# A two-pass third product for the half block of a Winograd matmul, with the operand sums moved to later steps

## The chip, the cores and the metric

The kernel runs on one core of a Trainium2 chip. A core has a matrix engine (TensorE, PE in the profile; its weight loads are PEld), a vector engine (VectorE, DVE), a scalar engine (ScalarE, ACT), GpSimd (POOL) and a sync engine (SP) that mostly issues DMAs. Each engine runs its own instructions in the order in which they are issued, and engines wait for each other through semaphores. The metric is the device time of one execution in microseconds (us), lower is better. The time before is the median of 3 runs.

## The reference, cut to what matters

```
xn = layernorm(x)                                     # x: (2048, 640)
A  = Cr @ (xn @ Dr.T) - Ci @ (xn @ Di.T)              # DFT over both axes, real part
h  = layernorm(xn)
u  = gelu(h.T @ w1 + b1)                              # (640, 1728)
y  = (u @ w2 + b2).T                                  # (2048, 640)
out = x + A + y
```

All inputs are fp32. The change lies in the last product, y = w2.T @ u.T: 2048 rows of output, 640 columns, and a contraction over 1728 = 13 blocks of 128 rows and half a block of 64.

## The kernel before, in words

**Three passes.** A fp32 operand a is split into a high part a_h (ScalarE, `high`, L138, rounding to the type that TensorE multiplies in one pass) and a low part a_l = a - a_h (VectorE, `low`, L141). A product is then three matmuls into the same PSUM bank (`three`, L149, L150, L152): w_h by m_h, w_h by m_l, w_l by m_h. If the low part of the weights is given as `None`, the third is left out.

**Winograd form.** Each large product is done as a 2 x 2 block product with seven multiplications instead of eight. In `row_steps` (L767) the weights A11, A12, A21, A22 come from HBM by DMAs on the SP queue, and the moving operands (combinations of the blocks B) lie ready in SBUF. VectorE forms four sums of the weights: S1 = A21 + A22, S2 = S1 - A11, S3 = A11 - A21, S4 = A12 - S2. The products, in the order of their steps: P1 (weights A11), P5 (S1), P6 (S2), P2 (A12), P7 (S3), P3 (S4), P4 (A22). One pass over these seven makes two row blocks of the result and is called a row step here. P1, P6, P7 and P4 add into one PSUM bank, P5 and P3 into a second, and P2 has a third; after each product the state of its bank is read out ("P1 out" is the reading after P1; L854 on ScalarE where it is copied, L841 on VectorE where it is added to what was read before). So P6 may begin only once P1 is out, P7 once P6 is out, P4 once P7 is out, P3 once P5 is out.

**The last product in two halves.** The contraction blocks 0 to 13 are paired as (f, f + 7). The first half (`down0`, 8 row steps) takes pairs 0 to 3, the second (`down1`, 8 row steps) pairs 4 to 6; its moving operand is called `sdown` in both, and its three pairs make 9 matmuls per product, 128x128 weights by 128x320. Block 13 has only 64 valid rows. The host gives its weights twice, in rows 0 to 63 and again in rows 64 to 127. For P2 and P4, whose second operand is zero in the missing rows, this is used ("stacked"): the weights' upper 64 rows hold the low part of the lower 64, the high part of the moving operand is repeated there and its low part is zero there, so that two passes do the work of three (8 matmuls instead of 9). `cut_piece` (L170) then makes two low operations, one of 64x128 that writes into the high tile and one of 128x256. `tail_rows` (L724) prepares the moving side once, as jobs in the first half. In S1 the upper rows of the last block need a copy of A21's (L789), since A22's are the repeated ones.

**Order.** Everything is issued in an order written out by hand, in turns (`turn_of`): turn i issues in this order the loads, the readings of product i - 1, the sums, the high part for product i + 2, extras, jobs, the low part for product i + 2, what is in `behind_lo`, and the matmuls of product i. `s0` is the turn of P1. Before, S1 and S3 are issued at turn s0 - 2 ahead of P1's low part, S2 at s0 - 1, S4 at s0 + 2. S1 has a slot of its own ("s"); S2 replaces A11, S3 replaces A21, S4 replaces A12. The first row step of the DFT product over the hidden axis (`s_hid`) already uses another order, the one of the `if s0 == s_hid` branch: S1 behind P1's low part at s0 - 2, S2 in the place of S1 at s0, S3 at s0 + 1, S4 at s0 + 2.

**The last row step** does not add to the output by DMA; it has the output rows loaded and adds them while reading out, so P1, P5 and P6 are read by VectorE (L850) instead of ScalarE, and P4 in two halves (L846).

Of the kernel before, what the change touches and what calls it, by code (L numbers as in the profile page):

```python
# [8 lines left out]
F32 = mybir.dt.float32  # L9
R32 = mybir.dt.float32r  # L10
BF16 = mybir.dt.bfloat16
AF = mybir.ActivationFunctionType
ALU = mybir.AluOpType

P = 128
# [6 lines left out]
TAIL = F - NF * P  # L22
# [47 lines left out]
def fnet_plus_mixer(  # L70
# [30 lines left out]
    nc = tc.nc  # L101
# [35 lines left out]
    def high(hi, src):  # L137
        nc.scalar.activation(hi, src, AF.Copy)  # L138
# [4 lines left out]
    def sub(to, a, b):  # L143
        nc.vector.tensor_sub(to, a, b)  # L144
# [20 lines left out]
    loads, sums, reads, extras, timed, behind_lo = (defaultdict(list) for _ in range(6))  # L165
# [558 lines left out]
    def tail_rows():  # L724


        v = []

        def get():
            v.append(place["x2"]()[P - TAIL :])  # L730
            nc.sync.dma_start(v[0], part_up[NF2 - 1][:TAIL])

        def piece(row, n):
            return v[0][:, row, n * H2 : (n + 1) * H2]

        def second(which, i):
            return moving["down1", 2][P - TAIL :, which, i, :]

        def job1():
            high(second(0, 1), piece(1, 0))  # L740
            sub(piece(0, 1), piece(0, 1), piece(0, 0))

        def job2():
            sub(piece(1, 1), piece(1, 1), piece(0, 1))
            sub(piece(1, 0), piece(1, 0), piece(1, 1))

        def job3():
            high(second(0, 5), piece(1, 0))
            nc.gpsimd.memset(second(1, 5).bitcast(F32), 0.0)

        return get, [(job1,), (job2,), job3]

# [14 lines left out]
    def row_steps(stage, nq, load_piece, at, end, bias=(None, None), base=None, earliest=0, each=None, aside={}, tail=False, stacked=()):  # L767
# [6 lines left out]
        s0, n = len(steps), nq * P  # L774
        raw, banks, held = {}, {}, {}

        def load(*names):
            for name in names:
                raw[name] = raw_slot(n)
                load_piece(raw[name], int(name[1]) - 1, int(name[2]) - 1)  # L780
# [47 lines left out]
        def read(i):  # L828
# [34 lines left out]
                    end(held["c"])  # L863
            return run

        for e, names in loads_of.items():
            loads[max(s0 + e, earliest)].append(lambda names=names: load(*names))
        if s0 == s_hid:


            operand[6] = "s"
            behind_lo[s0 - 2].append(first_sum)
            sums_of = {
                0: (lambda: sub(raw["s"], raw["s"], raw["A11"]),),
                1: (lambda: sub(raw["A21"], raw["A11"], raw["A21"]),),
                2: (lambda: sub(raw["A12"], raw["A12"], raw["s"]),),
            }
# [7 lines left out]
    def collect(c, ts):  # L885
        for i in range(2):
            nc.gpsimd.dma_start(out_rows[ts[i]], c[:, i, :], accum_op=ALU.add)

    def hidden(n, t, earliest):
        ts = (t, t + 4)  # L890

        def load_piece(to, i, j):
            c, b = divmod(ts[i], CH // P)
            nc.sync.dma_start(to.rearrange("p (j t) -> p j t", j=ND), y_part[j][c][:, :, b * P : (b + 1) * P])

        return row_steps("hid", ND, load_piece, ("ca", "cb")[n % 2], lambda c: collect(c, ts), earliest=earliest)

    def up(stage, r, at):
# [54 lines left out]
        if tail:  # L953
            aside += (7, 4)
        s0 = row_steps(
            f"up{stage}", 4, load_piece, at, end, earliest=s_up - 4, aside={i: by_dram(i) for i in aside}, tail=tail,
        )
        return s0

    def down(stage, t, at):  # L960
        f0, nq = (0, 4) if stage == 0 else (4, 3)
        ts = (t, t + NS // 2)
        last = stage == 1 and t == NS // 2 - 1

        def load_piece(to, i, j):
            f = f0 + NF2 * j
            nc.sync.dma_start(to, w2[ts[i], :, f * P : (f + nq) * P])

        def each(c, row, half, whole, at=slice(0, H2), queue=nc.sync):
            if whole:  # L970
                queue.dma_start(out_rows[ts[row]][:, half * H2 : (half + 1) * H2][:, at], c[:, at])

        held = []

        def before():

            held.append(place["v"]())
            for i in range(2):
                nc.sync.dma_start(held[0][:, i, :], out_rows[ts[i]])

        if last:
            loads[len(steps) - LOADS].append(before)
        bias = [b2_sb[:, i : i + 1] if stage == 0 else None for i in ts]
        return row_steps(
            f"down{stage}", nq, load_piece, at, lambda c: collect(c, ts), bias, (lambda: held[0]) if last else None,
            each=each if last else None, stacked=(2, 4) if stage else (),
        )


# [14 lines left out]
    s_hid = len(steps)  # L1004
# [29 lines left out]
    for t in range(NS // 2):  # L1034
        down(0, t, ("cb", "x1")[t % 2])
# [7 lines left out]
    for t in range(NS // 2):  # L1043
        down(1, t, ("ca", "cb")[t % 2])
# [88 lines left out]
```

## Time and profile before

| | |
|---|---|
| median of 3 runs | 875.51 us (875.5 to 876.32) |
| profiled execution, its own time | 875.92 us |
| its span | 874.2 us |
| TensorE busy | 869.0 us, 99%, 4924 matmuls |
| VectorE busy | 711.7 us, 81% |
| ScalarE busy | 530.2 us, 61% |
| GpSimd busy | 126.2 us, 14% |
| granted TensorE clock | 0.999 |

The page lists the busy time of each engine, the chain of work that ended last, and groups of instructions by line, operation and tile, with the mean of one and the idle time before them. A matmul's listed duration runs from its start to the end of its pipeline, so matmuls overlap in the list and their spacing is shorter than their duration. In a timeline each row has a start and a duration in us, the engine, the line, the operation, what it writes and reads, and in brackets how long its engine was idle before it and what ended that.

### The profile page before, as it was taken

What the parts mean: (1) busy time and instruction counts of PE and PEld (TensorE: products, weight loads), DVE (VectorE), ACT (ScalarE), POOL (GpSimd) and SP (SyncE); (2) the same over time, 40 slices, a digit from 0 to 9 for tenths busy, and PEclk for the clock granted to TensorE, in tenths of its full rate; (3) what the DMA queues carried; (4) which work ended last, traced back from release to release, by engine and by line L of the source; (5) the groups of instructions that cost most, each with busy time, mean ns of one, the idle gap of its engine ahead of it and who ended that gap; (6) DMA issues with size and microseconds to landing.
All of it is one profiled execution on the core that took longest, in us unless ns stands there. A gap on an engine that the chain in (4) does not pass through costs nothing.

```text
span 874.2 us, 13999 instructions
## 1 busy us (share of the span) xinstructions
PE 869.0 (99%) x4924; PEld 793.1 (91%) x4924; DVE 711.7 (81%) x1217; ACT 530.2 (61%) x960; POOL 126.2 (14%) x170
## 2 busy tenths in 40 slices
PE   9999999999999999999999999999999999999998
PEld 6888888888888888889999999999999999999998
DVE  7878878795887978788887787998678978897887
ACT  5746576764556566557565556675577766555553
POOL 0110100101121111222010101000212221111211
PEclk9999999999999999999999999999999999999999
DMA  7771554619385556869666756454678797766786
GB/s 270 231 266 76 194 203 132 242 59 357 54 219 92 163 119 133 208 92 195 168 127 166 156 139 196 162 177 138 142 170 181 169 244 193 190 136 133 151 173 139
DMA packets 86087, 147.64 MB, mean 169 GB/s; under 512 B 8512, under 2 KB 35904, under 8 KB 85760
## 3 DMA queue, kind: packets, MB, share of 16 engines
q1 hardware_dynamic: 64928, 95.80, 34.0%
q0 software_dynamic: 20800, 50.70, 30.6%
q8 instruction: 38, 0.62, 0.3%
q14 instruction: 33, 0.27, 0.1%
q10 hardware_dynamic: 288, 0.25, 0.1%
HBM read 99.96 MB, written 52.00 MB: 174 GB/s over the span
## 4 chain that ended last, share of the span: by engine, by line
PE 94%; DVE 3%; ACT 1%; DMA 1%; issue 1%; DVEq 0%; ACTq 0%
PE psum L149 30%; PE psum L150 30%; PE psum L152 29%; PE psum L477 5%; DVE piece L141 1%; DMA pieces<-y 1%; DVE pieces L144 0%; DMA x<-in_x 0%; ACT piece L138 0%; ACT n L259 0%; ACT x L259 0%; DVE pair L144 0%; DVE st L210 0%; DVE pieces L785 0%; DVE shid L141 0%
## 5 line engine op out<-in xcount | busy, mean ns | idle before, releaser
L141 DVE TENSOR_TENSOR piece<-pieces,piece 128x512 fp32r<-128x512 f32 (+2 forms) x524 | 350.1, 671 | 125.8 <-ACT piece L138 119.1
L138 ACT ACTIVATE piece<-pieces 128x512 fp32r<-128x512 f32 (+3 forms) x508 | 318.1, 627 | 212.0 <-PE psum L152 143.5
L150 PE MATMUL psum<-piece,n 128*128 128x512 f32 x504 | 196.4, 390 | 0.0
L149 PE MATMUL psum<-piece,n 128*128 128x512 f32 x504 | 196.2, 389 | 0.0
L152 PE MATMUL psum<-piece,n 128*128 128x512 f32 x504 | 196.1, 389 | 0.0
L149 PE MATMUL psum<-sup,piece 128*128 128x320 f32 x392 | 121.2, 310 | 0.0
L149 PE MATMUL psum<-sdown,piece 128*128 128x320 f32 x392 | 121.0, 309 | 0.0
L150 PE MATMUL psum<-sup,piece 128*128 128x320 f32 x392 | 120.9, 309 | 0.0
L150 PE MATMUL psum<-sdown,piece 128*128 128x320 f32 x392 | 120.9, 309 | 0.0
L152 PE MATMUL psum<-sup,piece 128*128 128x320 f32 x376 | 116.6, 310 | 0.0
L152 PE MATMUL psum<-sdown,piece 128*128 128x320 f32 x376 | 116.2, 309 | 0.0
L144 DVE TENSOR_TENSOR pieces<-pieces 128x512 f32<-128x512 f32 (+3 forms) x142 | 112.7, 794 | 2.6
L150 PEld LDWEIGHTS psum<-piece,n 128*128 128x128 f32 x504 | 94.6, 188 | 21.0 <-DVE piece L141 1.5
L149 PEld LDWEIGHTS psum<-piece,n 128*128 128x128 f32 x504 | 94.6, 188 | 19.9
L152 PEld LDWEIGHTS psum<-piece,n 128*128 128x128 f32 x504 | 94.6, 188 | 19.3
L152 PE MATMUL psum<-shid,piece 128*128 128x320 f32 x280 | 86.6, 309 | 0.1
L150 PE MATMUL psum<-shid,piece 128*128 128x320 f32 x280 | 86.5, 309 | 0.0
L149 PE MATMUL psum<-shid,piece 128*128 128x320 f32 x280 | 86.5, 309 | 0.0
L854 ACT ACTIVATE pair<-psum 128x320 f32<-128x320 f32 x102 | 44.5, 436 | 54.6 <-PE psum L152 49.8
L149 PEld LDWEIGHTS psum<-sup,piece 128*128 128x128 f32 x392 | 73.6, 188 | 0.6 <-ACT pairs L854 0.3
L149 PEld LDWEIGHTS psum<-sdown,piece 128*128 128x128 f32 x392 | 73.6, 188 | 0.2 <-ACT pair L852 0.2
L150 PEld LDWEIGHTS psum<-sup,piece 128*128 128x128 f32 x392 | 73.6, 188 | 0.0
(106 smaller groups left out, 1115.8 us busy)
## 6 DMA issues: line engine op xcount, KB each, us to landing
pieces<-in_dft_seq SPq DMA_DIRECT2D x128, 256.0 KB, 5.4
pieces<-in_w SPq DMA_DIRECT2D x88, 256.0 KB, 3.7
y<-c POOLq DMA_DIRECT2D x84, 256.0 KB, 6.1
out<-pair POOLq DMA_DIRECT2D x38, 320.0 KB, 5.3
pieces<-y SPq DMA_DIRECT2D x32, 320.0 KB, 3.9
pieces<-in_w SPq DMA_DIRECT2D x32, 192.0 KB, 3.1
out<-in_x SPq DMA_DIRECT2D x16, 320.0 KB, 7.1
up<-pair POOLq DMA_DIRECT2D x8, 640.0 KB, 3.2
```

What stands on the lines that cost most here:

```text
L138: nc.scalar.activation(hi, src, AF.Copy)
L141: nc.vector.tensor_sub(lo, src, hi.bitcast(F32))
L144: nc.vector.tensor_sub(to, a, b)
L149: nc.tensor.matmul(psum, wh, mh, start=first, stop=False, skip_group_check=True)
L150: nc.tensor.matmul(psum, wh, ml, start=False, stop=last and wl is None, skip_group_check=True)
L152: nc.tensor.matmul(psum, wl, mh, start=False, stop=last, skip_group_check=True)
L477: nc.tensor.matmul(banks[m, j], channels(k, j)[rows], w[cols], start=n == 0 and k == begin, stop=n == 2 and k == end, skip_group_check=True,)
L854: nc.scalar.activation(c, b, AF.Copy)
```

## The change

In `down1`, P3 becomes stacked too, beside P2 and P4. Three things go with it. On the moving side, `tail_rows` repeats the high part of P3's operand in the upper rows and clears its low part there. On the weight side, S4's upper rows in the last block must repeat its lower rows; A12's already do, so the upper rows of S2 in the last block are overwritten with its lower ones on ScalarE (`second_time`, 64x128, turn s0 + 1), after P6's parts have been cut from S2 and before S4 is formed. And the sums of `down1` take the order of the `s_hid` branch: S1 behind P1's low part, S2 in the place of S1 at turn s0 instead of in the place of A11 at s0 - 1, S3 at s0 + 1 instead of s0 - 2, S4 from the slot "s". The line numbers of the changed kernel are up to 8 higher.

```diff
         def job1():
             high(second(0, 1), piece(1, 0))
+            high(second(0, 2), piece(1, 1))
             sub(piece(0, 1), piece(0, 1), piece(0, 0))
...
         def job3():
             high(second(0, 5), piece(1, 0))
-            nc.gpsimd.memset(second(1, 5).bitcast(F32), 0.0)
+            for i in (2, 5):
+                nc.gpsimd.memset(second(1, i).bitcast(F32), 0.0)
...
+        if stacked:
+
+            def second_time():
+                last = raw["s"][:, n - P :]
+                nc.scalar.activation(last[TAIL:], last[:TAIL], AF.Copy)
+
+            extras[s0 + 1].append(second_time)
         for e, names in loads_of.items():
             loads[max(s0 + e, earliest)].append(lambda names=names: load(*names))
-        if s0 == s_hid:
-
+        if s0 == s_hid or stacked:
 
             operand[6] = "s"
             behind_lo[s0 - 2].append(first_sum)
             sums_of = {
                 0: (lambda: sub(raw["s"], raw["s"], raw["A11"]),),
                 1: (lambda: sub(raw["A21"], raw["A11"], raw["A21"]),),
                 2: (lambda: sub(raw["A12"], raw["A12"], raw["s"]),),
             }
...
-            each=each if last else None, stacked=(2, 4) if stage else (),
+            each=each if last else None, stacked=(2, 3, 4) if stage else (),
```

## The prediction

> **What bounds the kernel now.** First the page: the span, the busy times, the chain that ended last, and one costly group of the stage that is changed.
>
> ```profile
> span 874.2 us, 13999 instructions
> PE 869.0 (99%) x4924; PEld 793.1 (91%) x4924; DVE 711.7 (81%) x1217; ACT 530.2 (61%) x960; POOL 126.2 (14%) x170
> ...
> PE 94%; DVE 3%; ACT 1%; DMA 1%; issue 1%; DVEq 0%; ACTq 0%
> ...
> L152 PE MATMUL psum<-sdown,piece 128*128 128x320 f32 x376 | 116.2, 309 | 0.0
> ```
>
> TensorE carries the chain. The 309 ns of a matmul is not what removing one saves, since matmuls overlap. Second, then, the busy time in a stretch of the changed stage (columns: stretch, sum, then PE, PEld, DVE, ACT, POOL, clock, DMA):
>
> ```profile
> 810.00:820.00 10.00, 10.00 (x70) 10.00 (x69) 8.39 (x20) 5.67 (x14) 1.87 (x3) 1.00 0.81 159
> ```
>
> PE has no gap at the full clock, and VectorE is 84% busy: little room if its work comes in a chain. Third, the timeline of one row step, VectorE and then ScalarE (start, duration):
>
> ```profile
> 805.44 0.49 DVE L841 TENSOR_TENSOR pair<-psum,pair 128x320 f32<-128x320 f32 x1
> 805.84 0.55 DVE L785 TENSOR_TENSOR pieces<-pieces 128x384 f32<-128x384 f32 x1
> 806.42 0.22 DVE L789 COPY pieces<-pieces 64x128 f32<-64x128 f32 x1
> 806.68 0.56 DVE L144 TENSOR_TENSOR pieces<-pieces 128x384 f32<-128x384 f32 x1
> 807.16 0.55 DVE L141 TENSOR_TENSOR piece<-pieces,piece 128x384 fp32r<-128x384 f32 x1
> 807.63 0.48 DVE L841 TENSOR_TENSOR pair<-psum,pair 128x320 f32<-128x320 f32 x1
> 808.03 0.55 DVE L144 TENSOR_TENSOR pieces<-pieces 128x384 f32<-128x384 f32 x1
> 808.49 0.55 DVE L141 TENSOR_TENSOR piece<-pieces,piece 128x384 fp32r<-128x384 f32 x1
> 809.23 0.56 DVE L141 TENSOR_TENSOR piece<-pieces,piece 128x384 fp32r<-128x384 f32 x1 [0.18 <-ACT piece L138]
> 810.13 0.73 DVE L141 TENSOR_TENSOR piece<-pieces,piece 64x128 fp32r<-64x128 f32 x2 [0.34 <-ACT piece L138]
> 810.89 0.56 DVE L144 TENSOR_TENSOR pieces<-pieces 128x384 f32<-128x384 f32 x1
> ...
> 813.24 0.48 DVE L841 TENSOR_TENSOR pair<-psum,pair 128x320 f32<-128x320 f32 x1
> 813.74 0.73 DVE L141 TENSOR_TENSOR piece<-pieces,piece 64x128 fp32r<-64x128 f32 x2
> 814.38 0.49 DVE L841 TENSOR_TENSOR pair<-psum,pair 128x320 f32<-128x320 f32 x1
> ```
> ```profile
> 805.43 0.53 ACT L138 ACTIVATE piece<-pieces 128x384 fp32r<-128x384 f32 x1 [0.74 <-PE psum L152]
> ...
> 808.67 0.53 ACT L138 ACTIVATE piece<-pieces 128x384 fp32r<-128x384 f32 x1 [0.31 <-DVE pieces L144]
> 809.25 0.44 ACT L854 ACTIVATE pair<-psum 128x320 f32<-128x320 f32 x1
> ```
> ```profile
> 807.73 0.31 PE L149 MATMUL psum<-sdown,piece 128*128 128x320 f32 x1
> ```
>
> 805.44 and 814.38 are P7 out in two successive row steps: 8.94 us for 61 matmuls, 0.1466 us each. In order VectorE shows: P7 out, S1, its copy, S3, P1's low part, P3 out, S2, low parts of P5, P6, P2 (a pair), S4 and, further on, P2 out, P4's low pair, P7 out. ScalarE shows P1's high part, P6's high part, P1 out. 807.73 is P1's first matmul. So today S1, S3 and S2 are all made before P6's high part is asked for.
>
> **The change, part by part.**
>
> *Matmuls.* One third pass fewer in each of 8 row steps, with its weight load: 8 x 0.1466 = -1.17 us. A row step becomes 60 x 0.1466 = 8.80 us of PE. The Trainium skill, TensorE: Matmul & The Clock Gate, section Back-to-back issue gap, gives N/2.4 + 2.5 ns, which for 320 columns is 136 ns; by it the saving would be 1.09 us, and the measured spacing decides.
>
> *Setup.* One more high part (64x320) and one more fill, once, before the stage.
>
> ```profile
> L749 POOL MEMSET sdown<- x1: 687/687/687, 788.0 to 788.0; 64x320 f32 x1
> ```
> ```profile
> 798.44 0.86 POOL L887 DMA_DIRECT2D out<-pairs  x1 [9.73 <-DVE pairs L841]
> ```
> ```profile
> L138 ACT ACTIVATE sdown<-pairs x14: 461/727/733, 644.9 to 791.3; 128x640 fp32r<-128x640 f32 x9, 128x320 fp32r<-128x320 f32 x3, 64x320 fp32r<-64x320 f32 x2
> ```
>
> POOL's second 0.69 us comes ahead of output DMAs for which POOL idles 9.73 us anyway. ScalarE's extra 0.46 us falls before 791.3; it is 61% busy over the span, and the stage that first needs the result begins at about 799 (eight row steps of 8.94 before the last matmul at about 870.4). Both cost 0; without that cover, 1.15 us together. No DMA is added. The SP queue is passed by nothing: A12's next load overwrites A11, whose last reader comes a turn sooner.
>
> *ScalarE's new copy (64x128, 8 times).* Not in this trace. Above it lies 128x256; below it, what 128 columns add from one width to the next.
>
> ```profile
> L138 ACT ACTIVATE piece<-pieces 128x384 fp32r<-128x384 f32 x56 | 29.2, 522 | 20.6 <-PE psum L152 13.8 <-DVE pieces L144 3.4 <-ACT piece L138 2.6
> L138 ACT ACTIVATE piece<-pieces 128x256 fp32r<-128x256 f32 x4 | 1.6, 411 | 0.0
> ```
>
> 128 columns add 0.11, so 0.41 - 0.11 = 0.30 us; bounds 0.11 and 0.41. I take 0.30, the straight line through both rows. It waits for P6's low part, and queued behind it on ScalarE are P5 out, P7's high part, P6 out, P3's high part. S4, which needs the copy, starts 1.24 us after that low part ends (0.47 + 0.57 + 0.76 - 0.56, steps below), so at either bound the copy is hidden. Above 1.2 us it would hold S4.
>
> *The later sums.* This is what costs. S2 now overwrites S1's slot, so it can start only after P5's low part has read it, and P6's parts only after S2. A row step of the first product already has this order:
>
> ```profile
> 406.06 0.82 DVE L141 TENSOR_TENSOR piece<-pieces,piece 128x640 fp32r<-128x640 f32 x1 [0.15 <-ACT piece L138]
> 406.92 0.82 DVE L144 TENSOR_TENSOR pieces<-pieces 128x640 f32<-128x640 f32 x1
> 408.61 0.83 DVE L141 TENSOR_TENSOR piece<-pieces,piece 128x640 fp32r<-128x640 f32 x1 [0.86 <-ACT piece L138]
> ```
> ```profile
> 407.84 0.74 ACT L138 ACTIVATE piece<-pieces 128x640 fp32r<-128x640 f32 x1 [0.83 <-DVE pieces L144]
> 408.48 0.42 ACT L854 ACTIVATE pair<-psum 128x320 f32<-128x320 f32 x1
> ```
>
> S2 starts 0.03 after the low part's end, ScalarE 0.09 after S2, the low part 0.03 after ScalarE, and P1 out stands behind that high part. With 384 columns the steps form a closed loop over a row step, start to start: P1 low to S1 0.47 (the spacing of two unhindered operations, 807.16 to 807.63); S1 to copy 0.58; copy to P5's high part 0.22 + 0.09 = 0.31; to P5's low part 0.53 + 0.03 = 0.56; to S2 0.55 + 0.03 = 0.58; to P6's high part 0.55 + 0.09 = 0.64; to its low part 0.56; to S3 0.47; to P2's low pair 0.57 (behind 813.24 the pair waits for the whole operation); to S4 0.76; to P3's high part 0.56 + 0.09 = 0.65; to P3's low pair 0.55; to P2 out 0.64 (as 813.74 to 814.38; splitting P3's low part adds 0.17); to P4's pair 0.50; to P7 out 0.64; to the next P1 low 0.40. Sum 8.88 us against PE's 8.80.
>
> So the loop, not PE, sets the steady row step. P6 adds into P1's bank, so its first matmul waits for P1 out, and P1 out now stands behind P6's high part. Counted from P3's first matmul (17 before 807.73, so 805.24): P1's high part 0.19, its low part 0.56 later, P6's high part 3.14 later (the six steps above), P1 out 0.43 after that (408.48 - 407.84, less the 0.21 by which the high part is shorter), done 0.44 later: 4.76. P6 is due 34 matmuls on, at 4.98, its second matmul at 5.13. In the case at 863.86 below, the second matmul follows such an end by 0.38, which allows 5.14 here: just in time when the loop starts on time. The first row step has longer turns before it and loses nothing; the second uses up what slack there is; five to six later ones lose 0.08 each: **+0.4 us**.
>
> *The last row step.* Here P1, P5 and P6 are read out by VectorE (L850), in the same queue as the loop.
>
> ```profile
> 862.91 0.56 DVE L141 TENSOR_TENSOR piece<-pieces,piece 128x384 fp32r<-128x384 f32 x1 [0.19 <-ACT piece L138]
> 863.38 0.48 DVE L850 TENSOR_TENSOR pair<-psum,pair 128x320 f32<-128x320 f32 x1
> ...
> 865.88 0.49 DVE L850 TENSOR_TENSOR pair<-psum,pair 128x320 f32<-128x320 f32 x1
> ```
> ```profile
> 864.04 0.36 PE L149 MATMUL psum<-sdown,piece 128*128 128x320 f32 x1
> 864.24 0.31 PE L150 MATMUL psum<-sdown,piece 128*128 128x320 f32 x1
> ```
>
> P1 out ends at 863.86; P6's stretched first matmul loses 0.05, its second starts 0.38 after that end. Today P6's low part starts 1.13 before P6 is due; in the new order only about 0.4 (the loop, 0.1 late). P1 out then runs from 0.07 to 0.55 after the due time, P6's second matmul at 0.93 where 0.15 was due: 0.78 lost. P7 waits for P6 out in the same way. On VectorE from P1 out: S3 0.40, P2's pair 0.57, P5 out 0.64, S4 0.40, P7 low 0.47, P6 out 0.47, done 0.49 later: 3.51 after P6's due time, P7's second matmul 3.89, against 0.78 + 1.32 + 1.17 + 0.15 = 3.42: 0.47 more. Less the 0.05 of today: **+1.2 us**.
>
> Sum against the profiled execution's own 875.92 us: -1.17 + 0 + 0 + 0.4 + 1.2 = +0.43, 876.35. That execution is 0.41 above the median 875.51, so **about 876.0 us**: no change, since a measurement here tells no less than 0.2%, 1.75 us.
>
> **The rivals.**
>
> *The saving stays.* If S2 need not wait for the whole low part, or handovers are shorter, the loop falls below 8.80 and the last row step alone gives back part: 874.3 (all of it kept) to 875.3. For it: at 864.04 only 0.05 is lost today. Against: the first product's rows above. Chance 0.14.
>
> *Slower.* Three times in the loop ScalarE waits for VectorE (before the high parts of P5, P6, P3), and in the changed order for more than one engine at once. If each handover took 0.07 more than 0.09, the loop would be 9.09, and six row steps and the last would lose 0.2 each: 877.4. It decides from 0.18 per row step. For it: no row shows such a handover with a third wait. Against: 406.92 ends at 407.74, and 407.84 starts 0.10 later. Chance 0.13.
>
> *The clock falls.* Small stalls at every row step, PE queueing for a bank each time, bring the granted clock to half: a row step at half clock is 8.8 us longer, so from 885 up. Against: one stall of this kind is in the trace already, at the full clock.
>
> ```profile
> 703.72 0.34 PE psum L149
> 700.00:710.00 10.00, 10.00 (x69) 9.81 (x68) 7.15 (x13) 6.69 (x12) 2.28 (x3) 1.00 0.76 197
> ```
>
> Chance 0.01. The Trainium skill, same page, section A second HAM failure mode: psum-queue depth-cycling, describes such a loss; by this trace it does not happen.
>
> That the passes are not removed is excluded: the instruction order lists 8 matmuls fewer.
>
> **How the numbers follow.** My forecast has 0.70 (875.0 to 877.0 around 876.0), the saving 0.14, slower 0.13, the clock 0.01, and 0.02 is left for a gain beyond the removed matmuls. Faster by over 0.2% is that last 0.02; slower 0.13 + 0.01 = 0.14; within 0.2% 0.84. The range reaches into both neighbours, half of each: 874.5 to 877.4.
>
> **What would show it.** Matmuls of L152 on sdown 376 to 368. Steady row steps of 8.85 to 8.95, with small gaps at P6's first matmul released by P1 out; VectorE above 86% in 810 to 820. In the last row step gaps of about 0.8 at P6 and 0.5 at P7. Setup without PE gaps before 799. The prediction is wrong if row steps are 8.80 throughout, if the last one has no such gaps, or if PE waits elsewhere, for P2's or P3's low parts.

## The result and the profile after

| | before | after |
|---|---|---|
| median, 14 runs each | 875.64 us | 877.74 us |
| lowest to highest | 875.33 to 876.83 | 876.99 to 878.03 |
| ratio after / before, 95% interval | | 1.0019 [1.0013, 1.0026] |
| profiled execution, its own time and span | 875.92, 874.2 | 877.79, 876.0 |

By the medians the changed kernel is 2.1 us slower, 0.24%. The ratio in the table, 1.0019, lies a little below the quotient of the two medians; it is just inside the 0.2% taken as no change, its interval reaches beyond that, and the whole interval lies above 1. The forecast was about 0.5 us more than before; 877.74 lies 0.34 above the upper end of the range.

The page of the changed kernel, first the span and busy times, then the summary of the chain that ended last, then two groups of the changed product (mean of one, idle time before them):

```profile
span 876.0 us, 14002 instructions
...
PE 868.3 (99%) x4916; PEld 791.8 (90%) x4916; DVE 713.8 (81%) x1225; ACT 532.1 (61%) x969; POOL 126.6 (14%) x171
...
PE 87%; DVE 7%; ACT 3%; issue 2%; DMA 1%; DVEq 0%; ACTq 0%
...
L152 PE MATMUL psum<-sdown,piece 128*128 128x320 f32 x368 | 113.7, 309 | 0.0
...
L149 PEld LDWEIGHTS psum<-sdown,piece 128*128 128x128 f32 x392 | 73.6, 188 | 2.7 <-ACT pieces L872 0.8
```

The eight third passes are gone: 368 instead of 376. But VectorE's share of the chain rises from 3% to 7%, and L149's weight loads, which begin each product, wait 2.7 us. The same group of before:

```profile
L149 PEld LDWEIGHTS psum<-sdown,piece 128*128 128x128 f32 x392 | 73.6, 188 | 0.2 <-ACT pair L852 0.2
```

The stretches of time say where (columns: stretch, sum, PE, PEld, DVE, ACT, POOL, clock, DMA):

```profile
810.00:820.00 10.00, 10.00 (x69) 9.84 (x68) 8.50 (x20) 6.28 (x16) 2.09 (x3) 1.00 0.84 158
860.00:870.00 10.00, 9.19 (x61) 8.63 (x60) 8.96 (x22) 4.16 (x9) 1.73 (x2) 1.00 0.60 98
```

The last row step (second line) loses most, yet a steady one also has room between weight loads, at the full clock. Its timeline, VectorE, then ScalarE, then TensorE:

```profile
818.06 0.56 DVE L144 TENSOR_TENSOR pieces<-pieces 128x384 f32<-128x384 f32 x1
819.27 0.56 DVE L141 TENSOR_TENSOR piece<-pieces,piece 128x384 fp32r<-128x384 f32 x1 [0.65 <-ACT piece L138]
819.74 0.55 DVE L144 TENSOR_TENSOR pieces<-pieces 128x384 f32<-128x384 f32 x1
820.33 0.73 DVE L141 TENSOR_TENSOR piece<-pieces,piece 64x128 fp32r<-64x128 f32 x2
821.16 0.56 DVE L144 TENSOR_TENSOR pieces<-pieces 128x384 f32<-128x384 f32 x1
...
824.10 0.48 DVE L843 TENSOR_TENSOR pair<-psum,pair 128x320 f32<-128x320 f32 x1
```
```profile
818.71 0.53 ACT L138 ACTIVATE piece<-pieces 128x384 fp32r<-128x384 f32 x1 [0.95 <-DVE pieces L144]
819.14 0.42 ACT L856 ACTIVATE pair<-psum 128x320 f32<-128x320 f32 x1
...
820.00 0.31 ACT L872 ACTIVATE pieces<-pieces 64x128 f32<-64x128 f32 x1
...
821.75 0.53 ACT L138 ACTIVATE piece<-pieces 128x384 fp32r<-128x384 f32 x1
```
```profile
819.63 0.39 PE L149 MATMUL psum<-sdown,piece 128*128 128x320 f32 x1
819.86 0.30 PE L150 MATMUL psum<-sdown,piece 128*128 128x320 f32 x1
...
824.56 0.31 PE L150 MATMUL psum<-sdown,piece 128*128 128x320 f32 x1
824.73 0.39 PE L149 MATMUL psum<-sdown,piece 128*128 128x320 f32 x1
824.95 0.30 PE L150 MATMUL psum<-sdown,piece 128*128 128x320 f32 x1
```

VectorE runs S2 (818.06), P6's low part, S3, P2's pair, S4; ScalarE starts P6's high part at 818.71, 0.09 after S2's end, and P1 out (819.14) stands behind it. Matmul starts further apart than 0.147 us are TensorE's gaps: 0.08 at P6 (819.63 to 819.86), whose bank P1 out frees, and 0.10 at P4 (824.56 to 824.95), which waits for P7 out (824.10 to 824.58, VectorE). A steady row step takes 8.98 us, 0.18 more than its 60 matmuls. The last row step, TensorE:

```profile
864.69 0.31 PE L152 MATMUL psum<-sdown,piece 128*128 128x320 f32 x1
865.57 0.39 PE L149 MATMUL psum<-sdown,piece 128*128 128x320 f32 x1 [0.58 <-DVE pair L852]
865.80 0.30 PE L150 MATMUL psum<-sdown,piece 128*128 128x320 f32 x1
...
867.99 0.31 PE L150 MATMUL psum<-sdown,piece 128*128 128x320 f32 x1
868.53 0.39 PE L149 MATMUL psum<-sdown,piece 128*128 128x320 f32 x1 [0.23 <-DVE pair L852]
868.75 0.31 PE L150 MATMUL psum<-sdown,piece 128*128 128x320 f32 x1
```

Gaps of 0.82 at P6 and 0.47 at P7, both released by VectorE's reading L852. All gaps of the changed stage add to 2.57 us, against 0.05 before: 2.52 - 1.17 = +1.35. The stage's own length agrees: from its first matmul to the end of its last it runs from 798.78 to 870.56 before and from 799.30 to 872.43 now, which is 1.35 longer.

The rest of this execution's +1.87 is there before the stage begins (0.52). It arises at about 423 us, in the DFT product over the hidden axis, which the change leaves as it was. TensorE waits there for a low part:

```profile
423.12 0.31 PE L150 MATMUL psum<-shid,piece 128*128 128x320 f32 x1
424.09 0.41 PE L152 MATMUL psum<-shid,piece 128*128 128x320 f32 x1 [0.67 <-DVE piece L141]
```

Behind that stands VectorE's wait for a DMA into the weights, at this row step's S1, first before and then in the changed kernel:

```profile
417.88 0.83 DVE L785 TENSOR_TENSOR pieces<-pieces 128x640 f32<-128x640 f32 x1 [0.83 <-DMA pieces<-y]
```
```profile
418.49 0.82 DVE L787 TENSOR_TENSOR pieces<-pieces 128x640 f32<-128x640 f32 x1 [1.46 <-DMA pieces<-y]
```

The gaps near 423 us add to 0.94 in this execution and 0.34 in the profiled one of before, a difference of 0.6, of which 0.52 is left where the stage begins. The run `before_again` below shows that they can be long in the unchanged kernel too. That they also explain why the medians lie 2.1 apart and not 1.35 is an argument from single traces and is not shown.

### The profile page after: what moved, and what is told of

Its sections match the earlier page's. It is cut to its first block, busy times and chain, and to the rows that moved or that the text cites. A ratio compares the mean times of both kernels' runs of the same rounds, so it can differ in the third digit from the quotient of the medians.

```text
span 876.0 us, 14002 instructions
## 1 busy us (share of the span) xinstructions
PE 868.3 (99%) x4916; PEld 791.8 (90%) x4916; DVE 713.8 (81%) x1225; ACT 532.1 (61%) x969; POOL 126.6 (14%) x171
## 4 chain that ended last, share of the span: by engine, by line
PE 87%; DVE 7%; ACT 3%; issue 2%; DMA 1%; DVEq 0%; ACTq 0%
PE psum L149 27%; PE psum L150 27%; PE psum L152 27%; PE psum L477 5%; DVE piece L141 3%; ACT piece L138 1%; DVE pieces L144 1%; DMA pieces<-y 1%; DVE pieces L787 1%; DVE pair L843 1%; DMA x<-in_x 0%; ACT pair L856 0%; ACT n L259 0%; ACT pieces L872 0%; ACT x L259 0%
## 5 line engine op out<-in xcount | busy, mean ns | idle before, releaser
L141 DVE TENSOR_TENSOR piece<-pieces,piece 128x512 fp32r<-128x512 f32 (+4 forms) x532 | 351.0, 662 | 124.6 <-ACT piece L138 117.0
L149 PE MATMUL psum<-piece,n 128*128 128x512 f32 x504 | 196.2, 389 | 0.0
L152 PE MATMUL psum<-piece,n 128*128 128x512 f32 x504 | 196.1, 389 | 0.0
L149 PE MATMUL psum<-sdown,piece 128*128 128x320 f32 x392 | 122.0, 312 | 0.9 <-DVE pair L852 0.8
L149 PE MATMUL psum<-sup,piece 128*128 128x320 f32 x392 | 121.1, 310 | 0.0
L152 PE MATMUL psum<-sup,piece 128*128 128x320 f32 x376 | 116.5, 310 | 0.0
L152 PE MATMUL psum<-sdown,piece 128*128 128x320 f32 x368 | 113.7, 309 | 0.0
L149 PEld LDWEIGHTS psum<-piece,n 128*128 128x128 f32 x504 | 94.6, 188 | 19.7
L152 PEld LDWEIGHTS psum<-piece,n 128*128 128x128 f32 x504 | 94.6, 188 | 19.4
L152 PE MATMUL psum<-shid,piece 128*128 128x320 f32 x280 | 86.7, 309 | 0.7 <-DVE piece L141 0.7
L149 PE MATMUL psum<-shid,piece 128*128 128x320 f32 x280 | 86.5, 309 | 0.0
L149 PEld LDWEIGHTS psum<-sdown,piece 128*128 128x128 f32 x392 | 73.6, 188 | 2.7 <-ACT pieces L872 0.8
L149 PEld LDWEIGHTS psum<-sup,piece 128*128 128x128 f32 x392 | 73.6, 188 | 0.5 <-ACT pairs L856 0.3
L150 PEld LDWEIGHTS psum<-sdown,piece 128*128 128x128 f32 x392 | 73.6, 188 | 0.0
```

Source lines behind the costliest of these rows:

```text
L141: nc.vector.tensor_sub(lo, src, hi.bitcast(F32))
L149: nc.tensor.matmul(psum, wh, mh, start=first, stop=False, skip_group_check=True)
L150: nc.tensor.matmul(psum, wh, ml, start=False, stop=last and wl is None, skip_group_check=True)
L152: nc.tensor.matmul(psum, wl, mh, start=False, stop=last, skip_group_check=True)
```

## The experiments

The theory: the later sums cost time in two places, the steady row step, where VectorE, ScalarE and their handovers form a loop longer than 8.80 us, and the last row step, where VectorE's readings stand in that loop. The rivals: the cost belongs to the stacking of P3 itself (its copy on ScalarE, its split low part), or it lies outside the stage. Here are all runs in one table; the "account" is the stage's gaps less the 0.05 of before, less 1.17 where P3 has two passes.

| run | median, us | before beside it | ratio [95%] | steady row step, us | gaps in stage, us | account, us |
|---|---|---|---|---|---|---|
| stack_old_order | 876.18 | 876.21 | 0.9998 [0.9990, 1.0007] | 8.98 | 1.46 | +0.24 |
| order_only | 877.59 | 876.21 | 1.0017 [1.0008, 1.0025] | 8.95 | 1.19 | +1.14 |
| last_old | 876.63 | 876.21 | 1.0005 [0.9997, 1.0014] | 8.98 | 1.74 | +0.52 |
| s3_early | 875.61 | 876.21 | 0.9994 [0.9985, 1.0003] | 8.80 | 1.01 | -0.21 |
| s3_early_last_old | 875.53 | 876.01 | 0.9994 [0.9985, 1.0002] | 8.80 | 0.64 | -0.58 |
| s3_early_last_act | 876.55 | 876.01 | 1.0003 [0.9994, 1.0012] | 8.80 | 1.57 | +0.35 |
| after_again | 877.46 | 876.01 | 1.0014 [1.0005, 1.0023] | 8.98 | 2.55 | +1.33 |
| before_again | 876.26 | 876.01 | 1.0002 [0.9993, 1.0011] | 8.95 | 0.05 | 0 |
| s3_early_late_low | 875.64 | 875.80 | 0.9997 [0.9988, 1.0006] | 8.80 | 0.55 | -0.67 |
| no_copy (single execution) | 876.61 | 875.80 | | 8.98 | 2.24 | +1.02 |
| s3_early_last_copy (single execution) | 874.99 | 875.80 | | 8.80 | 0.28 | -0.94 |

Account and measured difference agree within about 0.5 us in every row. In the first comparison the same account gives +1.35 against the measured +2.1.

**stack_old_order: P3 in two passes, the sums where they were before.**

```diff
-                last = raw["s"][:, n - P :]
+                last = raw["A11"][:, n - P :]
...
-        if s0 == s_hid or stacked:
+        if s0 == s_hid:
```

> Two passes for P3, but the sums where they were: S1, S3 ahead of P1's low part, S2 in the place of A11, ScalarE's copy on A11's slot. Queue theory (VectorE and ScalarE form a closed loop that is longer than TensorE's row step, and the last row step loses time because its readings stand in VectorE's queue behind the later sums): the old order has its own tight place, P1's low part, which ends just as P1 starts; P3's split low part pushes it 0.17 us later while the row step gets 0.15 shorter, so most of the saving is lost in small gaps at P1, but the last row step stays whole: 874.8 to 876.0. Order rival (the later sums alone cost, two passes are free): 874.4, no gaps at all. Work rival (the added low part and the added copy cost, the order does not): as slow as the change, 877.7.

The time did not move. Its VectorE and then its TensorE show where the saving went:

```profile
815.75 0.56 DVE L144 TENSOR_TENSOR pieces<-pieces 128x384 f32<-128x384 f32 x1
816.23 0.55 DVE L141 TENSOR_TENSOR piece<-pieces,piece 128x384 fp32r<-128x384 f32 x1
```
```profile
816.62 0.31 PE L150 MATMUL psum<-sdown,piece 128*128 128x320 f32 x1
816.83 0.41 PE L152 MATMUL psum<-sdown,piece 128*128 128x320 f32 x1
```

S3 (815.75) stands ahead of P1's low part, which ends at 816.78, and P1's L152 starts at 816.83, 0.06 late; with the stretched matmul behind it 0.17 per row step. So without the new order the stacking saves nothing: P1's low part becomes the bound, at the same 8.98.

**order_only: the sums moved, P3 still in three passes.**

```diff
-        if s0 == s_hid:
+        if s0 == s_hid or stacked:
```

> The sums at their later steps, S2 in the place of S1, but P3 in three passes as before and no copy. Queue theory: a row step has 61 matmuls, 8.94 us, and the loop without the split low part is about 8.75, so steady row steps show no gaps; the last row step loses about 0.5 at P6 and 0.4 at P7: 876.5. Order rival: at least as slow as the change, 877.7 to 879. Work rival: 875.6, as before.

Steady row steps stay at 8.95 without gaps, but for one of 0.14 near 837 us: the loop hides behind 61 matmuls. The last row step pays, here VectorE and then TensorE:

```profile
863.72 0.56 DVE L141 TENSOR_TENSOR piece<-pieces,piece 128x384 fp32r<-128x384 f32 x1 [0.65 <-ACT piece L138]
864.19 0.48 DVE L850 TENSOR_TENSOR pair<-psum,pair 128x320 f32<-128x320 f32 x1
```
```profile
864.18 0.31 PE L152 MATMUL psum<-sdown,piece 128*128 128x320 f32 x1
864.82 0.38 PE L149 MATMUL psum<-sdown,piece 128*128 128x320 f32 x1 [0.34 <-DVE pair L850]
```

P1 out (864.19) stands behind P6's low part, which waited for ScalarE. The order alone costs 1.4 us; 1.05 of its 1.19 us of gaps lie there, at P6 and P7. The time is 1.1 above the expected 876.5; 0.6 of that is the before beside it, which stands at 876.21 and not at 875.6. By its time alone this run would also fit the rival that the order costs everything; the trace shows the cost in the last row step.

**last_old: the changed kernel, the last row step with the sums where they were.**

```diff
+                last = raw["A11" if base else "s"][:, n - P :]
...
+        if s0 == s_hid or stacked and not base:
```

> The change, with the last row step alone in the old order of sums (its copy on A11's slot). Queue theory: the gaps at P6 and P7 of the last row step, 1.3 us together in the changed kernel, go but for some 0.1 to 0.2; the seven steady row steps stay at 8.98: 876.4 to 876.7. Work rival: no change from the changed kernel, 877.7. A theory that puts the loss ahead of the stage (a DMA landing later in the first product): 877.7 less the last row step's part as well, so this run does not decide on it, but its trace shows the wait.

Gaps fall from 2.57 to 1.74, those of the last row step from 1.29 to 0.45; the ratio to before from 1.0019 and 1.0014 to 1.0005. Both places of the theory exist, and this undoes one of them.

**s3_early: S3 moved up, right behind S2.** If the loop is the bound, taking S3 out of the stretch behind P6's low part, where ScalarE waits for VectorE, and putting it where VectorE idles must shorten it.

```diff
-                0: (lambda: sub(raw["s"], raw["s"], raw["A11"]),),
-                1: (lambda: sub(raw["A21"], raw["A11"], raw["A21"]),),
+                0: (lambda: sub(raw["s"], raw["s"], raw["A11"]),)
+                + ((lambda: sub(raw["A21"], raw["A11"], raw["A21"]),) if stacked else ()),
+                1: () if stacked else (lambda: sub(raw["A21"], raw["A11"], raw["A21"]),),
```

> The change, with S3 issued right behind S2 in the same turn, so that VectorE makes it while it waits for ScalarE's high part of P6, where it idles 0.65 us in the changed kernel. Queue theory: the loop loses 0.47 us and falls from 8.98 to about 8.5, under TensorE's 8.80; steady row steps are 8.80 without gaps; in the last row step P6 still waits for P1's reading, about 0.5, and P7 for about 0.1: 1.3 plus 0.6 us better than the changed kernel, 875.4 to 876.2. Work rival: no change, 877.7, since no work is removed.

Its VectorE, from S1 of one row step to S1 of the next:

```profile
815.02 0.55 DVE L787 TENSOR_TENSOR pieces<-pieces 128x384 f32<-128x384 f32 x1
...
817.10 1.03 DVE L144 TENSOR_TENSOR pieces<-pieces 128x384 f32<-128x384 f32 x2
818.31 0.56 DVE L141 TENSOR_TENSOR piece<-pieces,piece 128x384 fp32r<-128x384 f32 x1 [0.18 <-ACT piece L138]
...
823.83 0.55 DVE L787 TENSOR_TENSOR pieces<-pieces 128x384 f32<-128x384 f32 x1
```

S2 and S3 run back to back (817.10, two of them) while ScalarE makes P6's high part; the idle time before P6's low part falls from 0.65 to 0.18, and the period from 8.98 to 8.81, which is TensorE's. That is the direct proof of the loop. The ratio to before is 0.9994, against 1.0014 to 1.0019 of the changed kernel; from before it can't be told apart.

**s3_early_last_old: both cures together.** The two diffs above in one kernel.

> The change with S3 right behind S2 in seven row steps (8.80 each, as shown by the run before) and the old order of sums in the last row step. Queue theory: the last row step's gap of 0.73 at P6 goes, its own gaps of some 0.45 (as seen with the last row step alone in the old order) come in its place: 0.3 better than S3 early alone, 0.9 faster than before, so 874.7 to 875.4 where before stands at 875.6 to 876.2. Rival (the last row step is limited by something else than VectorE's queue): no better than S3 early alone.

The gaps fall to 0.64, and the median is 0.48 under before, where 0.9 was expected; the interval takes in 1. By the account 0.58 of the 1.17 is kept.

**s3_early_last_act: the last row step's readings taken from VectorE.** This is `s3_early` with one thing more: P1, P5 and P6 of the last row step are copied by ScalarE, and GpSimd adds the output rows.

```diff
-                    nc.vector.tensor_add(c, b, base()[:, row, cols])
+                    nc.scalar.activation(c, b, AF.Copy)
+                    nc.gpsimd.tensor_add(c, c, base()[:, row, cols])
```

> The change with S3 right behind S2 in all eight row steps; in the last one P1, P5 and P6 are read by ScalarE as in the others, and GpSimd adds the output rows afterwards. Queue theory: nothing stands in front of the readings any more, the gaps at P6 and P7 of the last row step go, all eight row steps are 8.80: 0.7 better than S3 early alone, 1.2 faster than before less what is lost once at a ScalarE instruction near 836 (0.28): about -1.0. Rival (the last row step is limited by the sums' own chain): no better than S3 early alone. Against both stands only a slow addition on GpSimd, which then shows as a wait of VectorE for GpSimd.

The median is 0.54 above the before beside it, where 1.0 below it was expected. The gap at P6 went, and a new one of 1.1 us came at P7's third pass. VectorE, GpSimd and TensorE there:

```profile
863.86 1.15 DVE L141 TENSOR_TENSOR piece<-pieces,piece 64x128 fp32r<-64x128 f32 x2 [0.18 <-ACT piece L138]
865.11 1.04 DVE L144 TENSOR_TENSOR pieces<-pieces 128x384 f32<-128x384 f32 x1
```
```profile
863.55 0.87 POOL L853 TENSOR_TENSOR pair<-pair 128x320 f32<-128x320 f32 x1 [0.35 <-ACT pair L852]
864.70 2.19 POOL L853 TENSOR_TENSOR pair<-pair 128x320 f32<-128x320 f32 x2 [0.28 <-ACT pair L852]
```
```profile
866.22 0.31 PE L150 MATMUL psum<-sdown,piece 128*128 128x320 f32 x1
867.35 0.42 PE L152 MATMUL psum<-sdown,piece 128*128 128x320 f32 x1 [0.82 <-DVE piece L141]
```

While GpSimd adds, VectorE's pair takes 1.15 instead of 0.73 and S4 1.04 instead of 0.56; P7's low part is late for it. Taken one by one, S4 ends 0.42 after GpSimd's second add (866.16 and 865.74) and P7's low part 0.41 after its third (867.30 and 866.88), as if each had to wait for the add to end. The Trainium skill, GPSIMD Engine Reference, section Specifications, says that GpSimd shares its SBUF interfaces with VectorE and contends with VectorE instructions that have two SBUF inputs. These rows agree, and `s3_early_last_copy` below takes the adds away.

**after_again and before_again: the same two kernels once more, beside each other.** No edit.

> The changed kernel again, beside the others on one chip. Queue theory: the changed stage costs 1.4 us net (gaps of 2.6, less 1.17 of matmuls, less 0.05 of gaps before), so 1.4 over before in the mean; the rest of what was measured first, some 0.6, is the wait for a DMA of the first product, which differs from execution to execution and here lies anywhere between 0.3 and 0.9. Rival (the DMA wait belongs to the change): again 2 us over before, with a wait of 0.9 in the trace.

> The kernel before again, for a second trace. Queue theory: no gaps in the changed stage but 0.05 in the last row step; the wait for a DMA in the first product, 0.34 in the first trace, may be anything between 0.3 and 0.9. Rival (the DMA wait belongs to the change): 0.34 again, and equal times throughout.

The changed kernel is 1.45 slower than the before beside it, 1.2 slower than `before_again`; its gaps repeat (2.55). The wait near 423 us does not stay with a kernel. TensorE of `before_again`:

```profile
423.01 0.31 PE L150 MATMUL psum<-shid,piece 128*128 128x320 f32 x1
423.88 0.41 PE L152 MATMUL psum<-shid,piece 128*128 128x320 f32 x1 [0.56 <-DVE piece L141]
```

Its gaps there add to 0.82, in the first profile of before to 0.34, in `after_again` to 1.52, in `s3_early` to 0.26. VectorE's wait for the DMA at S1 is, in the same order, 1.32, 0.83, 2.01 and 0.76: what varies is when a DMA lands. These are single profiled executions, so whether the changed kernel meets a long wait more often is not settled; the first comparison's +2.1 against the second's +1.45 fits such a variation.

**s3_early_late_low: in the last row step the low parts of P6 and P7 behind the readings.** This too is `s3_early` with one thing more: the low operation of these two is issued one turn later, after that turn's reading (`top`, `bottom` are the high and low part).

```diff
...
+            if base and i in (6, 7):
+                late[e - 1] = bottom.real
+                bottom = bottom.later
...
+        for e, f in late.items():
+            reads[s0 + e].append(f)
```

> S3 right behind S2 in all row steps, and in the last row step VectorE reads P1 before it makes P6's low part, and P6 before P7's low part, so that the reading TensorE waits for comes first. Queue theory: of the 0.73 at P6 in the last row step 0.05 to 0.1 is left, and about as much comes at P7; with the 0.28 near 836 the gaps are 0.4 to 0.5 together, against 1.17 of matmuls saved: 0.7 to 0.8 faster than before. Rival (the sums' own chain limits the last row step): the gap at P6 stays above 0.5.

VectorE of the last row step:

```profile
862.97 0.48 DVE L856 TENSOR_TENSOR pair<-psum,pair 128x320 f32<-128x320 f32 x1
863.37 1.31 DVE L141 TENSOR_TENSOR piece<-pieces,piece 128x384 fp32r<-128x384 f32 x3
```

P1 out (862.97) now runs first. Of the gap at P6 0.10 is left, at its third pass, and 0.17 appears at P4; none is left at P7. The gaps are 0.55 together, with the 0.28 near 837 us. The median is 0.16 under before, within the noise, where 0.7 to 0.8 was expected.

**no_copy: the changed kernel without the copy on ScalarE.**

```diff
-            extras[s0 + 1].append(second_time)
```

> The change without ScalarE's new copy (left out, so that the upper rows of S4's last block hold something else; the third pass stays away). Queue theory: S4 no longer waits for two engines, which took 0.07 beyond the loop's 0.76, so the row step falls from 8.98 to about 8.91, not to TensorE's 8.80; the gaps at P6 and P4 shrink from 0.18 to 0.1 per row step, the last row step's gaps stay. Work rival (the copy's work costs): 8.80.

VectorE, S4 in two successive row steps:

```profile
820.25 0.56 DVE L144 TENSOR_TENSOR pieces<-pieces 128x384 f32<-128x384 f32 x1
...
829.22 0.56 DVE L144 TENSOR_TENSOR pieces<-pieces 128x384 f32<-128x384 f32 x1
```

Still 8.97: the copy is not part of the loop, and the expected fall to 8.91 did not come. S4 starts 0.07 sooner behind P2's pair (0.76 instead of 0.83), but ScalarE starts P3's high part 0.65 after S4's start instead of 0.59. In `order_only`, which has no copy either, that handover is the same, 0.09 from S4's end, and in the changed kernel it is only 0.03. So the way from P2's pair to P3's high part takes 1.41 without the copy and 1.42 with it. Why the second handover is short where S4 waits for the copy was not settled.

**s3_early_last_copy: as s3_early, the last row step's readings by ScalarE, and the addition of the output rows to P1, P5 and P6 left out.** This separates GpSimd's interference from the queue on VectorE.

```diff
-                    nc.vector.tensor_add(c, b, base()[:, row, cols])
+                    nc.scalar.activation(c, b, AF.Copy)
```

> S3 right behind S2, and in the last row step P1, P5 and P6 are read by ScalarE as in the other row steps; the addition of the output rows to these three is left out. Queue theory: no gap above 0.1 in the last row step, the row step 8.80 like the others; with GpSimd's additions gone VectorE's operations there have their usual lengths, 0.56 and 0.73. Rival (GpSimd had nothing to do with the slow VectorE operations): they stay above 1 us and the gap of 0.99 stays.

VectorE's pair and S4:

```profile
863.57 0.73 DVE L141 TENSOR_TENSOR piece<-pieces,piece 64x128 fp32r<-64x128 f32 x2 [0.18 <-ACT piece L138]
864.40 0.56 DVE L144 TENSOR_TENSOR pieces<-pieces 128x384 f32<-128x384 f32 x1
```

Back to 0.73 and 0.56 without GpSimd's adds, and no gap in the last row step. Both theories of that place hold: VectorE's queue made the gaps, and GpSimd made the new one. What is left is one gap of 0.28 near 837 us, and nearly the whole saving shows (874.99, a single execution).

## Why the prediction was right or wrong

**The direction was right, the size too small.** A change of less than 0.2% was forecast, and the result lies at that edge; the difference was to be +0.43 on the profiled execution, and came out as +1.87 there, +2.1 and +1.45 between medians. That the ratio, 1.0019, still lies inside 0.2% is luck: the gaps outside the last row step alone came out 0.9 us larger than forecast, which is half of the 0.2%. The rival "slower" (877.4) is nearer in time. Its stated cause, handovers 0.07 longer each, is not what happened, but its bound of 0.18 per row step was reached.

**Matmuls, -1.17:** right. 368 third passes, and where nothing holds it up (`s3_early`) a row step of 8.80.

**Setup, 0:** right; no new gap stands ahead of the stage.

**ScalarE's copy, 0.30 us, hidden:** right. It took 0.31 (L872, 820.00), and without it the row step stays 8.98.

**The loop, +0.4:** the mechanism right, the size wrong, and this is the step that failed: "The first row step has longer turns before it and loses nothing; the second uses up what slack there is; five to six later ones lose 0.08 each". The loop was summed as 8.88 and is 8.98. Of the 0.10, the largest term is P2's pair to S4, 0.83 instead of 0.76; S1's copy to P5's high part took 0.34 instead of 0.31; seven others took 0.01 more each; P3's high part gave back 0.06 (0.59 instead of 0.65). Those two terms at S4 nearly cancel, and `no_copy` moves both without changing the row step; what is left of the miss is the 0.03 and the seven of 0.01. With TensorE at 8.80 a miss of 1% on the sum more than doubles the excess, 0.08 to 0.18: outside the last row step the gaps are 2.57 - 1.29 = 1.28 instead of 0.4. Five row steps lose 0.17 to 0.19 each and one 0.09; the other 0.28 is the single wait near 837 us below.

**Where TensorE waits:** half right. P6, released by P1 out, was foreseen; P4, released by P7 out on VectorE, was not. It is the same loop, met at a second product: once the loop is late, each reading in it is late. One row step also has 0.28 more at P6 (837.86 in its timeline): ScalarE starts P6's high part 0.37 after S2's end instead of 0.09. The wait returns in most kernels with the new order, at 0.14 in `order_only`, where it is P5's high part that comes late, and not in `no_copy`. Counted from the start of each trace, the late one is the same ScalarE record, the 1472nd, in all ten traces with such a delay, also in `stack_old_order`, where the delay is hidden; in the other three another record stands there and no such delay is seen. So it goes with the place in ScalarE's stream and not with the later sums; its cause stays open.

**The last row step, +1.2:** right. 0.82 at P6 and 0.47 at P7 against 0.78 and 0.47. `order_only` and `last_old` show it from both sides, `s3_early_last_copy` that VectorE's queue makes it.

**What the sum left out:** the base was one profiled execution, in which the wait near 423 us was among the shortest. Of the +1.87, 0.52 comes from there. The other parts, -1.17 + 1.29 + 1.28 - 0.05, make 1.35, and with it 1.87.

**The rivals.** The saving does not stay, neither in the new order nor in the old one (`stack_old_order`). The clock stayed at 1.00 with gaps in every row step but the first. The Trainium skill, TensorE: Matmul & The Clock Gate, section A second HAM failure mode: psum-queue depth-cycling, describes a loss of clock for waits of this kind; this case does not show it. VectorE's share in 810 to 820 was 85%, not above 86%: it is bound by the handovers, not by its work.

## What to carry to other kernels

When TensorE is the bound by 1% only, taking matmuls away moves the bound to the chain that feeds it: sum that chain start to start over one period, handovers included, and treat an error of 1% of the sum as an error of the whole gain. Where two engines hand work to each other, fill the waiting engine's idle time with the independent operation (S3 behind S2) rather than putting it at its latest step behind the answer; that was worth 0.18 us per row step, more than the 0.15 of the removed pass. In a last iteration that reads its results on another engine than the others do, work out the order on that engine separately.

## What the runs showed of the hardware

- An add of two SBUF tensors on GpSimd (128x320, fp32) slowed VectorE's two-input operations beside it from 0.56 to 1.04 us and from 0.73 to 1.15. In two cases the slowed operation ended 0.41 to 0.42 after the end of an add. The three adds took 0.87, 1.04 and 1.18 themselves, all beside VectorE's work.
- In these traces a matmul that starts behind a wait is itself stretched: 0.38 to 0.42 instead of 0.31, and its successor starts 0.22 to 0.26 later instead of 0.147. Each small wait so costs 0.07 to 0.11 more than itself.
- Taking a dependency away did not shorten the loop: S4 without the copy started 0.07 sooner, and the next handover, from S4's end to ScalarE, grew from 0.03 to 0.09 (`no_copy`).
